# Weights in binary64 decoded with one VectorE pass less: the sign carried through ScalarE's parametric ReLU

## The chip, the cores and the metric

One core of a Trainium2 chip runs the whole program. The metric is device time in microseconds (us) of one execution; the kernel before was timed three times. Its engines are called PE (TensorE, matrix products; PEld are its weight loads), ACT (ScalarE), DVE (VectorE), POOL (GpSimd) and SP (SyncE, which here only issues DMAs).

## The reference

Attention in chunks of 64, then a feed-forward layer with a cosine gate. The weights come in binary64 (64-bit floats), the rest in 32-bit floats.

```python
# q, k, v: (8, 8, 576, 64) float32; chunks of 64 along the sequence
scores = scale * q_c @ k_c.T              # per chunk
scores = scores - max(scores)
attn = exp(scores); attn = attn / (sum(attn) + 1e-09)
out = attn @ v_c
x = out as (4608 tokens, 512)
h = x @ w_in                              # w_in (512, 2048) float64
g = h * cos(h)
return (g @ w_out).astype(float32)        # w_out (2048, 512) float64
```

## The kernel before

The 4608 tokens are nine tiles of 512. A tile's attention gives x, held as two parts (a rounded high part and the rest) so that TensorE's fast 32-bit format keeps the precision; weights and g are split in the same way. The feed-forward layer of one tile is 16 segments, one for each block of 128 of the 2048 hidden columns. A segment has two steps on PE: `hidden` (12 matmuls: 4 blocks of 128 inputs, three products of parts each) gives h, and `project` (12 matmuls) adds g times a block of w_out to four sums. `project` runs three segments (LAG) behind `hidden`.

Between them lies `activated`, six instructions on 128x512 numbers: L492 on ACT (the number of whole turns as an integer), L493 on DVE (h less these turns), L494 on ACT (Sin, which is the cosine by its bias), L495 on DVE (times h; this frees the bank of PSUM, of which there are two, so `hidden` of a segment waits for L495 of two segments earlier), L496 on ACT (high part), L497 on DVE (rest).

The weights, 16 blocks of w_in and 16 of w_out (128x512 each, 512 KB), are read by DMA as raw bits and turned into 32-bit floats on the chip, once, in `split_weight`. For each block: L243 on ACT multiplies the upper words, read as 32-bit floats, by 2 to the power -112, which rebases the exponent; L245 on ACT makes the three bits that come from the lower words (tile `half`); a first L238 pass on DVE shifts the upper word left by three, which pushes the sign out at the top, and joins these bits; a second L238 pass takes the sign from the raw upper word again and joins it; L254 on ACT rounds the high part; L259 on DVE subtracts for the rest. The tile `w` and the tile `half` have two buffers each, so a block's first passes wait for the block two before it.

A tile's attention in the first part (`early`): scores on PE (L177, tiles kt, qt), row maxima L317 and subtraction L321 on DVE, Exp on ACT (L371), sums L381 and reciprocal L385 and L386 on DVE, the product with the reciprocal on POOL or DVE (L391), transposes on PE (L400) with a copy on ACT (L406), the product with v on PE, and its split into x by L455 on ACT and L458 on DVE. Exp and Sin need different tables of ACT; a change of table is an ACT_TABLE_LOAD.

The order of the segments is tile 0's first eight, all of tile 1's, tile 0's last eight, and then tile by tile. For the first 32 segments, with the attention of tiles 0, 1 and 2, all decoding and all early DMA issues, the order is not written by hand: every piece of work is entered by `piece` in a list, with its engine, a length, what it follows, and the time at which its data arrives. `in_order` gives each a due time counted back from the matmul steps and tries 1500 random changes of these times; `placed` runs the list through with one piece at a time for each engine, and the order that ends earliest is issued. The engines then run their queues in that order; the real waits are semaphores. In that list the Sin of every segment follows the eight exponentials of tiles 0 and 1 (`raised`, L844), and the first one has the length 1.83 for its table. Behind the 32 segments the order is fixed by a loop (L855).

Of the kernel before, what the change touches and what calls it, by code (L numbers as in the profile page):

```python
# [11 lines left out]
F32 = mybir.dt.float32  # L12
# [20 lines left out]

EARLY = 2

BY_CHUNK = []

PAIRED = 9


# [4 lines left out]


PE, ACT, DVE, POOL, SP = range(5)

LONG = 2.0

# [6 lines left out]
def placed(work, after_it, rank):  # L57


    n = len(work)  # L60
    left = [len(w[3]) for w in work]
    ready = [w[4] for w in work]
    can = [[] for _ in range(5)]
    for i in range(n):
        if not left[i]:
            can[work[i][0]].append(i)
    free = [0.0] * 5
    starts = [0.0] * n
    slow = 0.0
    for _ in range(n):  # L70
        best = None
        for e, c in enumerate(can):
            if not c:
                continue
            near = 0.2 + min(max(free[e], ready[i]) for i in c)
            first = None
            for i in c:
                at = max(free[e], ready[i])
                if at <= near:

                    mine = (rank[i] if e != PE or work[i][1] > LONG else -1e9, at, i)
                    if first is None or mine < first:
                        first = mine
            if best is None or first[1] < best[0]:
                best = (first[1], first[2], e)
        at, i, e = best
        length = work[i][1]
        if e == PE:

            if at - free[e] > IDLE:  # L90
                slow = at + IDLE
            if length > LONG:
                length += max(0.0, min(length, slow - at))
        starts[i] = at
        free[e] = at + length
        can[e].remove(i)
        for j in after_it[i]:
            left[j] -= 1

            way = 0.0 if e == PE == work[j][0] and length > LONG else work[i][5] - work[i][1]  # L100
            ready[j] = max(ready[j], free[e] + way)
            if not left[j]:
                can[work[j][0]].append(j)
    return starts
# [38 lines left out]
def attention_then_cos_ffn(ctx: ExitStack, tc, qT, kT, v, w_in, w_out, out, wide):  # L143
# [25 lines left out]
    def kept(ins):  # L169
        tc.keep_in_program_order(ins)  # L170
        return ins
# [43 lines left out]
    def split_weight(name, fc, low):  # L215


        raw, n = w_raw.pop((name, fc))
        made = []

        def w():
            if not made:
                made.append(dec.tile([P, n], F32, name="w"))
            return made[0]

        nothing = lambda: None
        if not wide:
            pieces = [lambda: nc.gpsimd.tensor_copy(w(), raw[:, :n])] + [nothing] * 3
        else:

            both = raw.bitcast(U32)[:, : 2 * n].rearrange("p (n k) -> p n k", k=2)
            lower, upper = both[:, :, 0], both[:, :, 1]

            def joined(first, shift, op0, second):
                bits = w().bitcast(U32)
                kept(nc.vector.scalar_tensor_tensor(  # L238
                    bits, first or bits, shift, second or bits, op0=op0, op1=ALU.bitwise_or
                ))  # L240

            pieces = [
                lambda: kept(nc.scalar.activation(  # L243
                    w(), upper.bitcast(F32), AF.Copy, scale=2.0 ** -(MORE // 8))),
                lambda: kept(nc.scalar.activation(low, lower, AF.Copy, scale=LOWEST)),  # L245
                lambda: joined(None, 3, ALU.logical_shift_left, low),
                lambda: joined(upper, 1 << 31, ALU.bitwise_and, None),
            ]

        def high():  # L250
            o = SHIFT if name == "in" else 0
            parts = wts.tile([P, 2 * n + PAD], F32R, name=f"w_{name}{fc}")
            hi, lo = parts[:, o : o + n], parts[:, o + n : o + 2 * n]
            kept(nc.scalar.copy(out=hi, in_=w()))  # L254
            w_parts[name, fc] = (hi, lo)

        def rest():
            hi, lo = w_parts[name, fc]
            kept(nc.vector.tensor_tensor(lo, w(), hi.bitcast(F32), op=ALU.subtract))  # L259

        return pieces + [high, rest]
# [41 lines left out]
    def scores_early(t, hp, s):  # L303

        qt, kt = queries.pop((t, hp))
        for c in range(NCH):
            cs = slice(c * CH, (c + 1) * CH)
            for h in range(2):
                hs = slice(h * CH, (h + 1) * CH)
                matmul(s[hs, cs], qt[hs, cs], kt[hs, cs], start=True, stop=True)  # L310
        sv = s.rearrange("p (c k) -> p c k", k=CH)
        e = weights_of(t, hp // 2)[:, hp % 2]

        m = att.tile([P, NCH], F32, name="m", bufs=4)

        def largest():
            kept(nc.vector.tensor_reduce(out=m, in_=sv, op=ALU.max, axis=AX.X))  # L317

        def below():
            mb = m.unsqueeze(2).broadcast_to([P, NCH, CH])  # L320
            kept(nc.vector.tensor_tensor(e, sv, mb, op=ALU.subtract))  # L321

        def lowered():
            kept(nc.vector.tensor_scalar(m, m, -SCALE, None, op0=ALU.mult))

        def raised_and_summed():
            z = sums_of(t)[:, hp]
            for c in range(NCH):
                kept(nc.scalar.activation(
                    e[:, c], sv[:, c], AF.Exp, bias=m[:, c : c + 1], scale=SCALE,  # L330
                    accum_out=z[:, c : c + 1],
                ))

        return [largest, below, lowered, raised_and_summed]

    def scores(t, g, banks):

# [259 lines left out]

    work = []

    def piece(eng, length, run, *after, at=0.0, lag=0.15):  # L600
        work.append([eng, length, run, [a for a in after if a is not None], at, length + lag])
        return len(work) - 1

    arrival = [3.6]
# [45 lines left out]
    for i, (name, fc) in enumerate(turn_of):  # L650
        key = ("w", name, fc)
        made[key] = split_weight(name, fc, low_bits[i % 2])
        back = turn_of[i - 2] if i > 1 else None
        u = piece(ACT, 0.52, rest_of(key, 0), split.get(back), at=here[name, fc])
        l = piece(ACT, 0.52, rest_of(key, 1), joined.get(back), at=here[name, fc])
        joined[name, fc] = piece(DVE, 0.6, rest_of(key, 2), u, l)
        w = piece(DVE, 0.6, rest_of(key, 3), joined[name, fc])
        h = piece(ACT, 0.52, rest_of(key, 4), w)
        split[name, fc] = piece(DVE, 0.6, rest_of(key, 5), h)


    x_done = {}
    banks_free = {}
    turned_out = {}

    raised = []

    def early(t):
        s, e, z, q, w, p = {}, {}, {}, {}, {}, {}
        for hp in range(HP):  # L670
# [6 lines left out]
            )  # L677
            m = piece(DVE, 0.6, rest_of(key, 0), s[hp])
            room = turned_out.get((t - 1, hp // 2))
            if (t, hp) in BY_CHUNK:  # L680
                m = piece(DVE, 0.2, rest_of(key, 2), m)
                z[hp] = e[hp] = banks_free[which] = piece(ACT, 1.2, rest_of(key, 3), m, room)
            else:
                banks_free[which] = piece(DVE, 0.6, rest_of(key, 1), m, room)
                e[hp] = piece(ACT, 0.6, lambda hp=hp: exponentials(t, hp), banks_free[which])
            raised.append(e[hp])
        for hp in range(HP):
            if hp in z:
                continue
            z[hp] = piece(DVE, 0.6, lambda hp=hp: total(t, hp), e[hp], z.get(hp - 1))  # L690
        for a in (0, 2):
            i = piece(DVE, 0.45, lambda a=a: inverse(t, a, a + 2), z[a], z[a + 1])
            for hp in (a, a + 1):
                if t or hp < 2:
                    q[hp] = piece(POOL, 1.0, lambda hp=hp: quotient(t, hp, nc.gpsimd), i)
                else:
                    q[hp] = piece(DVE, 0.6, lambda hp=hp: quotient(t, hp), i)
        for hp in range(HP):
            key = ("t", t, hp)
            at = banks_free["a", hp % 2] if t else p.get(hp - 2)  # L700
# [36 lines left out]
    def attend_third(begin):  # L737
        t = 2
        below = []
        for g in range(2):  # L740
# [5 lines left out]
            for h in range(2):  # L746
                m = piece(DVE, 0.6, rest_of(key, 2 * h), s)
                below.append(piece(DVE, 0.6, rest_of(key, 2 * h + 1), m))
                banks_free["a", h] = below[-1]
        x = piece(ACT, 4.4, lambda: exponentials(t), *below)  # L750
        z = [None]
        for hp in range(HP):
            z.append(piece(DVE, 0.6, lambda hp=hp: total(t, hp), x, z[-1]))
        z = piece(DVE, 0.5, lambda: inverse(t), z[-1])
        q = [piece(DVE, 0.6, lambda hp=hp: quotient(t, hp), z) for hp in range(HP)]
        w = None
        for g in range(2):
            pts = []
# [40 lines left out]
    for s in range(STAGE):  # L799
# [39 lines left out]
            made[key] = activated(*order[s], made["h", s])  # L839
            made[key][0]()  # L840
        a = piece(ACT, 0.53, begin_g, hid, given.get(s - 2), lag=0.2)
        sine = 0.55 if s else 1.83
        for i, (eng, length) in enumerate(((DVE, 0.6), (ACT, sine), (DVE, 0.6), (ACT, 0.53), (DVE, 0.6)), 1):
            a = piece(eng, length, rest_of(key, i), a, *([projected.get(s - LAG)] if i == 4 else raised if i == 2 else ()))  # L844
            if i == 3:
                held[s] = a
        given[s] = a
# [75 lines left out]
```

## Time and profile before

| | us |
|---|---|
| median of 3 runs | 864.16 (863.83 to 865.03) |
| the profiled execution | 864.98 |
| its span, first to last instruction | 863.2 |
| PE busy (matmuls) | 844.5, 98% of the span |
| DVE busy | 573.9, 66% |
| ACT busy | 390.5, 45% |
| POOL busy | 8.0, 1% |
| granted TensorE clock, mean | 0.996 |
| DMA: packets' share of 16 engines | 18.7%, mean 67 GB/s |

Busy is time in which at least one instruction of the engine ran. A high share over the span tells which engine is the bound on the whole, not where it stands still: for that the span is cut into stretches, and each gap of PE is put beside what ended it. Two instructions of one engine overlap a little at their ends, so the distance between their starts is shorter than the duration of one. A granted clock of 1 is 2.4 GHz, 0.5 would be 1.2 GHz.

### The profile page before, as it was taken

The numbers are of one execution on the slowest core, as the hardware profiler recorded it, in microseconds if no ns is written. First come the engines' busy times: TensorE is split into PE (matmuls) and PEld (weight loads), VectorE is DVE, ScalarE is ACT, GpSimd is POOL, SyncE is SP. The second block draws the span as 40 slices with busy tenths as digits, with TensorE's granted clock in tenths as the row PEclk, the third lists the DMA queues.
The fourth block names the chain that finished last, engine by engine and source line by source line (L and its number), as shares of the span: only waits on it lengthen the run. The fifth ranks groups of instructions, "written<-read, shape, count | busy, mean of one in ns | idle before, by whom it ended". The sixth has DMA issues, their size and how long they took to land.

```text
span 863.2 us, 14114 instructions
## 1 busy us (share of the span) xinstructions
PE 844.5 (98%) x5792; PEld 694.9 (81%) x5792; DVE 573.9 (66%) x974; ACT 390.5 (45%) x632; POOL 8.0 (1%) x12
## 2 busy tenths in 40 slices
PE   5899999999999999999999999999999999999998
PEld 5677888888888888888888888888888888888886
DVE  6999998854696567665776568645865576644332
ACT  4888975343433335333533353334433353333332
POOL 1020000000000000000000000000000000000000
PEclk9999999999999999999999999999999999999999
DMA  9972200330103000300130010301030010001001
GB/s 345 416 314 97 75 1 1 123 123 2 49 1 123 25 20 31 123 25 2 49 113 15 22 49 19 104 25 50 1 122 25 2 50 25 1 1 49 1 1 49
DMA packets 26560, 57.53 MB, mean 67 GB/s; under 512 B 2944, under 2 KB 2944, under 8 KB 26496
## 3 DMA queue, kind: packets, MB, share of 16 engines
q1 hardware_dynamic: 26496, 56.63, 18.2%
q8 instruction: 45, 0.74, 0.4%
q14 instruction: 19, 0.16, 0.1%
HBM read 46.14 MB, written 10.49 MB: 66 GB/s over the span
## 4 chain that ended last, share of the span: by engine, by line
PE 92%; DMA 5%; DVE 2%; SPq 0%; issue 0%
PE acc L177 45%; PE h L177 43%; PE a L177 4%; DMA w_out<-in_w_out_dram 3%; DMA kt<-in_kT_dram 1%; DMA w_in<-in_w_in_dram 1%; DVE w L238 1%; DVE w_in L259 0%; SPq L174 0%; DVE g_lo L497 0%; DVE g L495 0%; DVE z L381 0%; DVE x L458 0%; DVE w_out L259 0%; DVE g L493 0%; PE a L400 0%
## 5 line engine op out<-in xcount | busy, mean ns | idle before, releaser
L177 PE MATMUL h<-x,w_in 128*128 128x512 f32 x1728 | 416.7, 390 | 1.9 <-DVE g L495 1.7
L177 PEld LDWEIGHTS h<-x,w_in 128*128 128x128 f32 x1728 | 324.7, 188 | 70.2 <-DVE g L495 2.1
L177 PE MATMUL acc<-w_out,g_hi 128*128 128x512 f32 x1152 | 358.2, 392 | 0.0
L177 PEld LDWEIGHTS acc<-w_out,g_hi 128*128 128x128 f32 x1152 | 214.0, 188 | 45.3
L177 PE MATMUL acc<-w_out,g_lo 128*128 128x512 f32 x576 | 224.4, 390 | 0.0
L493 DVE SCALAR_TENSOR_TENSOR g<-g,h 128x512 f32<-128x512 int32 x144 | 98.5, 684 | 138.9 <-ACT g L492 138.2
L492 ACT ACTIVATE g<-h 128x512 int32<-128x512 f32 x144 | 85.7, 595 | 194.8 <-PE h L177 194.3
L497 DVE TENSOR_TENSOR g_lo<-g,g_hi 128x512 fp32r<-128x512 f32 x144 | 99.8, 693 | 74.1 <-ACT g_hi L496 71.0
L496 ACT CAST g_hi<-g 128x512 fp32r<-128x512 f32 x144 | 89.4, 621 | 127.6 <-DVE g L495 81.3
L494 ACT ACTIVATE g<-g 128x512 f32<-128x512 f32 x144 | 91.1, 633 | 121.9 <-DVE g L493 121.8
L495 DVE TENSOR_TENSOR g<-h,g 128x512 f32<-128x512 f32 x144 | 99.3, 690 | 53.0 <-ACT g L494 49.8
L177 PEld LDWEIGHTS acc<-w_out,g_lo 128*128 128x128 f32 x576 | 108.1, 188 | 22.7
L417 DVE STREAM_TRANSPOSE pts<-e 32x256 f32<-32x256 f32 x224 | 97.2, 435 | 3.9
L177 PEld LDWEIGHTS a<-kt,qt 64*64 64x64 f32 x1024 | 18.8, 136 | 8.6 <-issue 6.7
L381 DVE TENSOR_REDUCE z<-e 128x8 f32<-128x512 f32 x36 | 23.8, 678 | 0.9 <-ACT e L371 0.9
L177 PE MATMUL a<-kt,qt 64*64 64x64 f32 x1024 | 21.1, 222 | 3.3 <-issue 1.6
L371 ACT ACTIVATE e<-e 128x1024 f32<-128x1024 f32 (+1 forms) x22 | 19.1, 897 | 10.5 <-DVE e L321 10.4
L238 DVE SCALAR_TENSOR_TENSOR w<-w,half 128x512 uint32<-128x512 uint32 x32 | 22.8, 712 | 0.0
L458 DVE TENSOR_TENSOR x<-a,x 128x512 fp32r<-128x512 f32 (+1 forms) x36 | 22.0, 653 | 0.5 <-ACT x L455 0.5
L177 PEld LDWEIGHTS a<-pts,vt 64*64 64x64 f32 x1056 | 17.2, 136 | 5.6 <-issue 4.6
L391 DVE TENSOR_TENSOR e<-e,z 128x512 f32<-128x512 f32 x30 | 20.2, 683 | 0.0
L362 DVE TENSOR_TENSOR e<-a,m 128x512 f32<-128x512 f32 x28 | 19.2, 686 | 0.5
(52 smaller groups left out, 269.5 us busy)
## 6 DMA issues: line engine op xcount, KB each, us to landing
qt<-in_qT_dram SPq DMA_DIRECT2D x36, 256.0 KB, 5.0
kt<-in_kT_dram SPq DMA_DIRECT2D x36, 256.0 KB, 5.3
vt<-in_v_dram SPq DMA_DIRECT2D x34, 256.0 KB, 3.4
w_in<-in_w_in_dram SPq DMA_DIRECT2D x16, 512.0 KB, 9.7
w_out<-in_w_out_dram SPq DMA_DIRECT2D x16, 512.0 KB, 10.0
out_dram<-w SPq DMA_DIRECT2D x16, 256.0 KB, 2.1
out_dram<-half SPq DMA_DIRECT2D x16, 256.0 KB, 2.0
out_dram<-x SPq DMA_DIRECT2D x4, 256.0 KB, 2.0
```

The lines of the kernel that those rows point to most:

```text
L177: kept(nc.tensor.matmul(*args, **kw))
L238: kept(nc.vector.scalar_tensor_tensor(bits, first or bits, shift, second or bits, op0=op0, op1=ALU.bitwise_or))
L381: kept(nc.vector.tensor_reduce(out=sums_of(t)[:, hp], in_=weights_of(t, hp // 2)[:, hp % 2], op=ALU.add, axis=AX.X))
L391: kept(eng.tensor_tensor(e, e, zb, op=ALU.mult))
L417: kept(nc.vector.transpose(out=dst[o : o + BL, :, qb], in_=src[i : i + BL, :, kb]))
L458: kept(nc.vector.tensor_tensor(lo, xq, hi.bitcast(F32), op=ALU.subtract))
L492: lambda: kept(nc.scalar.activation(n, h, AF.Identity, bias=0.25, scale=0.5 / math.pi)),
L493: lambda: kept(nc.vector.scalar_tensor_tensor(g, n, -2.0 * math.pi, h, op0=turns, op1=over)),
L494: lambda: kept(nc.scalar.activation(g, g, AF.Sin, bias=0.5 * math.pi)),
L495: lambda: kept(nc.vector.tensor_tensor(g, h, g, op=ALU.mult)),
L496: lambda: kept(nc.scalar.copy(out=g_hi, in_=g)),
L497: lambda: kept(nc.vector.tensor_tensor(g_lo, g, g_hi.bitcast(F32), op=ALU.subtract)),
```

## The change

The first ACT pass on the upper words becomes a parametric ReLU (Prelu) with the slope minus 2 to the power 32 for negative numbers. A negative weight comes out positive and with 32 added to its exponent, which sets a bit of the exponent that is free here. The shift by three then brings this bit to the place of the sign. So one pass of DVE joins everything, and the second L238 pass goes, for each of the 32 blocks.

The list of pieces changes too. Every entry gets two more fields. `table` names the table (Exp or Sin); `placed` adds 1.28 where a piece needs another than the one held. `port` marks work of POOL and DVE passes with two operands in SBUF; `placed` lets none of one engine start before the last of the other ends. The wait of the Sins on `raised` goes, with the fixed 1.83 and the 4.4 for tile 2's exponentials (now 1.92). An unused branch (`BY_CHUNK` is empty) is taken out.

```diff
 def placed(work, after_it, rank):
+    taken = {DVE: 0.0, POOL: 0.0}
+    table = AF.Exp
+    def soonest(e, i):
+        at = max(free[e], ready[i])
+        if work[i][6]:
+            at = max(at, taken[POOL if e == DVE else DVE])
+        return at
...
-            near = 0.2 + min(max(free[e], ready[i]) for i in c)
+            near = 0.2 + min(soonest(e, i) for i in c)
...
         length = work[i][1]
+        if work[i][7]:
+            length += TABLE * (work[i][7] != table)
+            table = work[i][7]
...
+        if work[i][6]:
+            taken[e] = free[e]
...
-            def joined(first, shift, op0, second):
+            def joined():
                 bits = w().bitcast(U32)
                 kept(nc.vector.scalar_tensor_tensor(
-                    bits, first or bits, shift, second or bits, op0=op0, op1=ALU.bitwise_or
+                    bits, bits, 3, low, op0=ALU.logical_shift_left, op1=ALU.bitwise_or
                 ))
             pieces = [
                 lambda: kept(nc.scalar.activation(
-                    w(), upper.bitcast(F32), AF.Copy, scale=2.0 ** -(MORE // 8))),
+                    w(), upper.bitcast(F32), AF.Prelu, scale=2.0 ** -(MORE // 8), alpha=-(2.0**32))),
                 lambda: kept(nc.scalar.activation(low, lower, AF.Copy, scale=LOWEST)),
-                lambda: joined(None, 3, ALU.logical_shift_left, low),
-                lambda: joined(upper, 1 << 31, ALU.bitwise_and, None),
+                joined,
             ]
...
+    def piece(eng, length, run, *after, at=0.0, lag=0.15, port=False, table=None):
+        port = port or eng == POOL
...
-        joined[name, fc] = piece(DVE, 0.6, rest_of(key, 2), u, l)
-        w = piece(DVE, 0.6, rest_of(key, 3), joined[name, fc])
-        h = piece(ACT, 0.52, rest_of(key, 4), w)
-        split[name, fc] = piece(DVE, 0.6, rest_of(key, 5), h)
+        joined[name, fc] = piece(DVE, 0.6, rest_of(key, 2), u, l, port=True)
+        h = piece(ACT, 0.52, rest_of(key, 3), joined[name, fc])
+        split[name, fc] = piece(DVE, 0.6, rest_of(key, 4), h, port=True)
...
-        sine = 0.55 if s else 1.83
-        for i, (eng, length) in enumerate(((DVE, 0.6), (ACT, sine), (DVE, 0.6), (ACT, 0.53), (DVE, 0.6)), 1):
-            a = piece(eng, length, rest_of(key, i), a, *([projected.get(s - LAG)] if i == 4 else raised if i == 2 else ()))
+        for i, (eng, length) in enumerate(((DVE, 0.6), (ACT, 0.55), (DVE, 0.6), (ACT, 0.53), (DVE, 0.6)), 1):
+            a = piece(eng, length, rest_of(key, i), a, *([projected.get(s - LAG)] if i == 4 else ()), port=i == 5, table=AF.Sin if i == 2 else None)
```

The products L391 on DVE are marked `port=True` as well, and the pieces with Exp (`early`, `attend_third`) get `table=AF.Exp`.

## Rows read from the trace of the kernel before

**Rows 1.** Windows: us, then busy of each engine (instructions), granted clock, DMA.
```profile
20.00:75.00 55.00, 47.70 (x470) 38.80 (x463) 53.30 (x89) 46.80 (x83) 5.22 (x4) 0.97 0.84 336
...
75.00:120.00 45.00, 45.00 (x258) 37.11 (x257) 44.65 (x74) 42.08 (x72) 0.00 (x0) 1.00 0.11 37
...
200.00:840.00 640.00, 640.00 (x4222) 526.43 (x4221) 397.65 (x676) 250.72 (x396) 0.00 (x0) 1.00 0.11 38
```
**Rows 2.** Timeline of PE: start, us, instruction, count; in brackets idle before, releaser.
```profile
28.64 6.85 PE L177 MATMUL h<-x,w_in 128*128 128x512 f32 x24
37.17 5.75 PE L177 MATMUL h<-x,w_in 128*128 128x512 f32 x24 [1.68 <-DVE g L495]
...
66.76 1.06 PE L400 MATMUL a<-ident,e 128*128 128x128 f32 x8 [2.11 <-DVE x L458]
```
**Rows 3.** Chain that ended last: start, us, what.
```profile
74.65 2.72 PE h L177 x12
```
**Rows 4.** Timeline of ACT, 33 to 37 us.
```profile
33.28 0.62 ACT L371 ACTIVATE e<-e 128x512 f32<-128x512 f32 x1
...
34.47 1.28 ACT L494 ACT_TABLE_LOAD   x1
35.77 0.63 ACT L494 ACTIVATE g<-g 128x512 f32<-128x512 f32 x1
```
**Rows 5.** Timeline of DVE, 22 to 37 us.
```profile
22.72 0.69 DVE L259 TENSOR_TENSOR w_in<-w,w_in 128x512 fp32r<-128x512 f32 x1
...
28.25 0.41 DVE L458 TENSOR_TENSOR x<-acc,x 128x256 fp32r<-128x256 f32 x1
...
29.30 1.29 DVE L238 SCALAR_TENSOR_TENSOR w<-w_in,w 128x512 uint32<-128x512 uint32 x2
30.51 0.68 DVE L317 TENSOR_REDUCE m<-a 128x8 f32<-128x512 f32 x1
...
36.43 0.69 DVE L495 TENSOR_TENSOR g<-h,g 128x512 f32<-128x512 f32 x1 [0.40 <-ACT g L494]
```
**Rows 6.** Groups over the span: count | busy us, mean ns | idle before.
```profile
L238 DVE SCALAR_TENSOR_TENSOR w<-w_in,w 128x512 uint32<-128x512 uint32 x16 | 11.5, 722 | 0.1
L238 DVE SCALAR_TENSOR_TENSOR w<-w_out,w 128x512 uint32<-128x512 uint32 x16 | 11.0, 687 | 0.3
```
**Rows 7.** Groups of DVE, 18 to 35 us (one row), 37.2 to 65.3 us (two rows).
```profile
L238 DVE SCALAR_TENSOR_TENSOR w<-w_in,w 128x512 uint32<-128x512 uint32 x4 | 2.7, 686 | 0.0
...
L238 DVE SCALAR_TENSOR_TENSOR w<-w_in,w 128x512 uint32<-128x512 uint32 x4 | 3.3, 827 | 0.0
L238 DVE SCALAR_TENSOR_TENSOR w<-w_out,w 128x512 uint32<-128x512 uint32 x3 | 2.1, 688 | 0.1
```
**Rows 8.** Groups of ACT, 20 to 75 us.
```profile
L243 ACT ACTIVATE w<-w_out 128x512 f32<-128x512 f32 x8 | 5.4, 674 | 0.0
L494 ACT ACTIVATE g<-g 128x512 f32<-128x512 f32 x8 | 5.1, 633 | 0.6 <-DVE g L493 0.6
...
L492 ACT ACTIVATE g<-h 128x512 int32<-128x512 f32 x8 | 4.8, 596 | 1.6 <-PE h L177 1.5
...
L496 ACT CAST g_hi<-g 128x512 fp32r<-128x512 f32 x7 | 4.4, 623 | 1.8 <-DVE g L495 1.8
L243 ACT ACTIVATE w<-w_in 128x512 f32<-128x512 f32 x6 | 4.0, 669 | 0.3 <-DVE w_in L259 0.3
...
L494 ACT ACT_TABLE_LOAD x1 | 1.3, 1283 | 0.0
```
**Rows 9.** Timeline of POOL (first two) and DVE.
```profile
12.78 2.04 POOL L391 TENSOR_TENSOR e<-e,z 128x512 f32<-128x512 f32 x2 [11.48 <-DVE z L386]
...
61.55 2.72 POOL L391 TENSOR_TENSOR e<-e,z 128x512 f32<-128x512 f32 x2 [5.41 <-DVE z L386]
...
63.29 1.53 DVE L259 TENSOR_TENSOR w_in<-w,w_in 128x512 fp32r<-128x512 f32 x1
...
65.34 1.27 DVE L458 TENSOR_TENSOR x<-a,x 128x512 fp32r<-128x512 f32 x2
```

More of the change, by code (lines that the diff above doesn't have):

```diff
@@ L34 @@
 EARLY = 2
-BY_CHUNK = []
 PAIRED = 9
@@ L47 @@
 PE, ACT, DVE, POOL, SP = range(5)
+TABLE = 1.28
 LONG = 2.0
@@ L74, in placed @@
                 continue
-            near = 0.2 + min(max(free[e], ready[i]) for i in c)
+            near = 0.2 + min(soonest(e, i) for i in c)
             first = None
             for i in c:
-                at = max(free[e], ready[i])
+                at = soonest(e, i)
                 if at <= near:
@@ L227, in split_weight @@
         if not wide:
-            pieces = [lambda: nc.gpsimd.tensor_copy(w(), raw[:, :n])] + [nothing] * 3
+            pieces = [lambda: nc.gpsimd.tensor_copy(w(), raw[:, :n])] + [nothing] * 2
         else:
@@ L321, in below @@
             kept(nc.vector.tensor_tensor(e, sv, mb, op=ALU.subtract))
[L323 to L334, printed above, removed]
+        return [largest, below]
     def scores(t, g, banks):
@@ L598, in attention_then_cos_ffn @@
     work = []
-    def piece(eng, length, run, *after, at=0.0, lag=0.15):
-        work.append([eng, length, run, [a for a in after if a is not None], at, length + lag])
+    def piece(eng, length, run, *after, at=0.0, lag=0.15, port=False, table=None):
+        port = port or eng == POOL
+        work.append([eng, length, run, [a for a in after if a is not None], at, length + lag, port, table])
         return len(work) - 1
@@ L664, in attention_then_cos_ffn @@
     turned_out = {}
-    raised = []
     def early(t):
@@ L679, in early @@
             room = turned_out.get((t - 1, hp // 2))
[L680 to L686, printed above, removed]
+            banks_free[which] = piece(DVE, 0.6, rest_of(key, 1), m, room)
+            e[hp] = piece(ACT, 0.6, lambda hp=hp: exponentials(t, hp), banks_free[which], table=AF.Exp)
         for hp in range(HP):
-            if hp in z:
-                continue
             z[hp] = piece(DVE, 0.6, lambda hp=hp: total(t, hp), e[hp], z.get(hp - 1))
@@ L696, in early @@
                 else:
-                    q[hp] = piece(DVE, 0.6, lambda hp=hp: quotient(t, hp), i)
+                    q[hp] = piece(DVE, 0.6, lambda hp=hp: quotient(t, hp), i, port=True)
         for hp in range(HP):
@@ L749, in attend_third @@
                 banks_free["a", h] = below[-1]
-        x = piece(ACT, 4.4, lambda: exponentials(t), *below)
+        x = piece(ACT, 1.92, lambda: exponentials(t), *below, table=AF.Exp)
         z = [None]
@@ L754, in attend_third @@
         z = piece(DVE, 0.5, lambda: inverse(t), z[-1])
-        q = [piece(DVE, 0.6, lambda hp=hp: quotient(t, hp), z) for hp in range(HP)]
+        q = [piece(DVE, 0.6, lambda hp=hp: quotient(t, hp), z, port=True) for hp in range(HP)]
         w = None
```

## The prediction

> **What bounds the kernel now.** I read the windows table first, because a mean over 863 us hides stages [rows 1]. From 200 to 840 us PE is busy 640.00 us of 640 at a granted clock of 1.00 (2.4 GHz): whatever VectorE (398 us) or ScalarE (251 us) does there costs nothing, and the tail behind it decodes no weight. So a gain can only come from the start. From 20 to 75 us PE is busy 47.7 of 55 us while VectorE is busy 53.3 and ScalarE 46.8. From 75 to 120 us VectorE is again full (44.65 of 45), but PE is full too, at full clock: the two engines run ahead there, and their work is not late. The stretch to argue from is 20 to 75 us.
>
> Next the timeline of PE, for its gaps, each with what ended it [rows 2]. h of segments 0 and 1 runs from 28.64 us in 6.85 us (two steps at full clock are 5.44 us, by the 2.72 us step of [rows 3]). PE then stands still for 1.68 us, until VectorE's L495 frees a bank at 37.1 us. The next long gap is 2.11 us, ends at 66.76 us, and is put down to VectorE's L458. From there to the tail the chain is steps of 2.72 us end to end. So what the change moves in time for the step at 74.65 us moves the end by as much, if no new gap opens behind it.
>
> Last, what stands behind the first gap, read backwards. L495 at 36.43 us needs the first Sin at 35.77 us, this needs its table (34.47 us, 1.28 us), and in the list of pieces this first Sin waits for all eight exponentials of tiles 0 and 1; the last of them runs at 33.28 us [rows 4]. That one needs L317 at 30.51 us and the L321 behind it, and ahead of these in VectorE's queue stand two sign passes, 1.29 us at 29.30 us, and the last quarter of tile 0's x at 28.25 us [rows 5]. PE had all of h0's weights at 23.4 us (L259 at 22.72 us), but it began at 28.64 us, as the last x came and tile 1's scores had been put ahead. VectorE's order, not DMA, sets the first 37 us.
>
> **The change, part by part.** *Sign passes.* 32 instructions of L238 go, 16 of 722 ns and 16 of 687 ns, 22.5 us of busy time in all [rows 6]. One pass costs its queue 0.60 us (two of them 1.29 us, less 0.69 us for one of such length [rows 5]), so 19.2 us of queue. Four stand in the queue from 18 to 35 us, 2.4 us; the two of 29.30 us, 1.2 us, are directly on the chain above. Between 37.2 and 65.3 us there are 4 + 3 = 7 more, 4.2 us [rows 7]. All behind 75 us are free of effect, being hidden by PE.
>
> *Prelu in place of Copy.* Same count, operands and scale; 32 instructions of ScalarE change their function. No Prelu is in the trace. The nearest rows: the Copy that it replaces, 669 and 674 ns, and the Sin of 633 ns [rows 8]. I take 0.67 us, the same operands being nearest, so nothing; the ends are 0.63 and, as far above, 0.71 us, and 14 of them in the stretch make 0.6 us either way, beside 8.2 us in which ScalarE is idle there (55 less 46.8). A Prelu needing its own table is a rival below.
>
> *The first Sin no longer waits for the exponentials; the list counts table loads itself.* The planner may now put it sooner, at the price of 2 more loads (2.57 us of ScalarE at 1283 ns [rows 8]), or still behind the exponentials. What h2 gains has two ends. The low end is the 1.2 us of passes on the chain. The high end is h0 at 23.4 us with Sin 0 at once: h0 and h1 take 6.85 us at their clock of today and end at 30.3; g0's chain after h0's 3.4 us (L492 0.60, then 0.69, load 1.28, Sin 0.63, 0.69: 3.9 [rows 8]) ends at 30.7; h2 there instead of at 37.17 is 6.5 us. Below nothing: one alternation on the chain, 2.57 less 1.2, 1.4 us lost. I take 3.0 us: the four sign passes (2.4 us, the chain being VectorE's queue for nearly all of it) plus some 0.6 us, one place in that queue, from L317, L321 and the late x no longer standing behind decoding work.
>
> *VectorE and GpSimd kept apart.* While GpSimd runs its pair of products from 61.55 us, a VectorE subtraction takes 1.53 us in place of 0.69, and the pair itself 2.72 us, not 2.04 as at 12.78 us [rows 9]. The list now starts no two-operand pass of VectorE beside it. Worth at the second gap: from 0.84 us saved ahead of L458 at 65.34 us to the same lost, if nothing else is ready for VectorE meanwhile. I take nothing.
>
> *The second gap.* VectorE reaches L458 4.2 us sooner by its 7 passes, PE needs it 3.0 us sooner by the first term. 1.2 us of difference come off 2.11; I take 1.0, as ScalarE feeds the same x (ends 0 and 2.1). What is late next there is ScalarE: a segment with two new weights costs it nine instructions, some 5.4 us at 0.60, against PE's 5.44.
>
> *The rest* (removed dead branch, lengths in the list for tile 2, number of empty pieces) issues nothing else on a queue, SP's loads included; the order of tile 2's exponentials and the partial sums may move, under a PE that is full from 75 us. Nothing.
>
> Sum: 3.0 + 1.0 = 4.0 us. The profiled execution took 864.98 us (span 863.2 and 1.78 around it), so 861.0; the median of the three runs is 0.82 us lower, 864.16, and the forecast made against it is 860.2 us.
>
> **The rivals.** *Larger* (0.16): h0 at 23.4 us and the whole 6.5 us, the second gap giving little (0.5): 857 us. For it: PE had its weights at 23.4 us, and the granted clock of 0.97 from 20 to 75 us would come back as its early gaps go. Against: ScalarE is 85% busy from 20 to 75 us and would have 8.2 us to spare for being 7 us ahead.
>
> *ScalarE takes over* (0.18): it loses no instruction. If it lets VectorE's time go to waste, only the 1.2 us on the chain stay: 863.0 us, no change. The same comes out of 3.0 + 1.0 with one alternation of tables on the path (2.57 us): 862.7 us. For it: 42.1 of 45 us busy from 75 us on. Against: of its idle 8.2 us, 1.8 end at L495, the largest share [rows 8].
>
> *Table loads, on the slower side* (0.05): from 20 to 75 us there are 14 Copies to be replaced and 8 Sins, and 1 load. If a Prelu is held by neither Exp's nor Sin's table, each Sin is followed by a load for the next Prelu and then one for itself: up to 16 loads, 20.5 us. ScalarE's 8.2 idle us hide six; from the seventh on PE waits; at 16 it is 12.3 us more, 876.5 us. Against: the Copy, casts and Identity run between Sins without a load in the trace, and these loads are only charged in the list for Exp and Sin.
> The Trainium skill, ScalarE: Activation LUTs (Table sets: the hidden batching unit), names relu, copy, identity and abs as in every set, and does not name the parametric one; its section What ACT_TABLE_LOAD costs gives 2.66 us for a switch, drain included. By that price 16 loads would come to 42.6 us and the time to 898.5 us. The trace disagrees on the drain: load at 34.47, Sin at 35.77 us, 1.30 us in all [rows 4].
>
> *The stretched order, slower* (0.07): tile 1's four products on GpSimd bar VectorE's two-operand passes for 4 x 1.02 us in the list; if nothing fills that, the x of tile 1 comes later than PE, now ahead, wants it, and the gap of 2.11 us grows by up to 4.1: less the 2.4 us of passes on the first chain, 865.9 us. It decides once more than 2.4 us of these 4.1 stay empty.
>
> **How the numbers follow.** Forecast 0.54, with its own range 858.4 to 862.3; larger 0.16; ScalarE 0.18; table loads 0.05; order 0.07. What a measurement of this kernel can tell from no change is about 0.2%, 1.7 us: faster is below 862.4, slower above 865.9. Faster 0.54 + 0.16 = 0.70; same 0.18; slower 0.05 + 0.07 = 0.12. The range runs from 856.5 (0.06 of the larger case lies below) to 864.8 (the two slower cases above, 0.12).
>
> **What would show it.** Right: 32 L238-like passes left, 32 Prelus of about 0.67 us, one table load from 20 to 75 us or at most three, h2 at 33 to 35 us, the step that was at 74.65 us starting near 70.6 us, VectorE below 95% from 20 to 75 us. Wrong: h2 at 36 us or later; PE gaps that now end at ScalarE (g_hi, pts, the weights' casts); loads between Sins; a gap of more than 2 us before tile 1's third transpose.

## The result: 0.2% slower, and the profile after

The changed kernel took 867.1 us (median of 20 runs, 865.39 to 868.54) against 865.14 us for before in the same runs: a ratio of 1.0021, 95% interval 1.0014 to 1.0028. The forecast was 860.2 us with a range up to 864.8, and faster. The profiled execution took 865.84 us, span 864.1 us, 0.9 us longer than before's 863.2. It is the third quickest of the 20; the rest of the 1.96 us between the two medians lies in executions that left no trace.

The first 75 us went as forecast, and better. Timeline of PE in the changed kernel (start, us, instruction; L193 is the old L177, L405 the old L400, L463 the old L458, L500 the old L495):

```profile
24.93 3.03 PE L193 MATMUL h<-x,w_in 128*128 128x512 f32 x12
...
28.97 3.02 PE L193 MATMUL h<-x,w_in 128*128 128x512 f32 x12
...
33.00 5.75 PE L193 MATMUL h<-x,w_in 128*128 128x512 f32 x24
...
60.69 1.22 PE L405 MATMUL a<-ident,e 128*128 128x128 f32 x8 [0.66 <-DVE x L463]
```

h of segment 0 begins 3.7 us sooner than in [rows 2], h2 is at 33.00 us, not 37.17, without a gap, and the second gap is 0.66 us, not 2.11. The chain has the step of [rows 3] (`hidden` of segment 8) at 68.69 us, 5.96 us sooner:

```profile
68.69 2.72 PE h L193 x12
```

The windows show where that went (columns as in [rows 1]). VectorE is down from 53.3 to 47.9 us from 20 to 75 us, PE up from 47.7 to 52.5. ScalarE is up from 46.8 to 52.55 us there. But from 120 to 200 us PE stands still for 4.84 us, and the granted clock of the stretch is 0.98; before had 80.00 of 80 us busy there (last row).

```profile
20.00:75.00 55.00, 52.45 (x492) 42.81 (x490) 47.87 (x81) 52.55 (x93) 4.77 (x4) 1.00 0.85 337
75.00:120.00 45.00, 45.00 (x316) 36.73 (x315) 40.06 (x66) 39.54 (x73) 0.00 (x0) 1.00 0.11 36
120.00:200.00 80.00, 75.16 (x442) 61.47 (x441) 49.99 (x90) 31.16 (x49) 0.00 (x0) 0.98 0.20 66
```
```profile
120.00:200.00 80.00, 80.00 (x529) 65.80 (x528) 59.67 (x106) 36.18 (x58) 0.00 (x0) 1.00 0.20 67
```

The gap stands in PE's timeline, with the steps ahead of it. The first row is tile 2's product with v (its first half), the next two are the last two hidden steps of tile 1:

```profile
147.62 1.16 PE L193 MATMUL a<-pts,vt 64*64 64x64 f32 x64
148.71 3.02 PE L193 MATMUL h<-x,w_in 128*128 128x512 f32 x12
...
154.30 2.88 PE L193 MATMUL h<-x,w_in 128*128 128x512 f32 x12
...
164.74 4.44 PE L193 MATMUL h<-x,w_in 128*128 128x512 f32 x12 [4.84 <-DVE g L500]
```

After the gap a step takes 4.44 us, not 2.72, at a granted clock of 0.65 for these microseconds (window, columns as above):

```profile
164.70:169.10 4.40, 4.36 (x12) 3.23 (x12) 3.30 (x6) 1.25 (x3) 0.00 (x0) 0.65 0.00 0
```

That is 1.72 us more. So 4.84 + 1.72 = 6.56 us are given back of 5.96, and some 0.3 us in small places make the 0.9 us of the spans.

What held L500 is read on ScalarE's timeline (L460 is the old L455, L497 to L502 are the old L492 to L497):

```profile
147.86 0.62 ACT L501 CAST g_hi<-g 128x512 fp32r<-128x512 f32 x1 [0.81 <-DVE g L500]
155.63 1.08 ACT L460 CAST x<-a 128x512 fp32r<-128x512 f32 x2 [7.15 <-PE h L193]
156.59 1.23 ACT L497 ACTIVATE g<-h 128x512 int32<-128x512 f32 x2
162.47 0.63 ACT L499 ACTIVATE g<-g 128x512 f32<-128x512 f32 x1 [4.66 <-DVE g L498]
```

The cast of tile 2's x has its input at 148.8 us, when the product ends. It starts at 155.63 us, in the middle of tile 1's last hidden step, and that step is named as what ended 7.15 us of idle time. `x_room` gives tile 2 the buffers named `x1`, where tile 1's x stands: the new x can be written only when the last hidden step of tile 1 has read the old one (the second experiment tests that this is the wait). L497 of segment 22 was ready at 151.7 us and stood behind the cast. VectorE's queue has its counterpart, two L463 and eight transposes, ahead of the L498 that L497 feeds. The chain of waits from there (start, us, what):

```profile
154.46 1.15 PE h L193 x5
...
156.11 0.60 ACT x L460
...
157.89 0.69 DVE x L463
...
161.75 0.69 DVE g L498
...
163.40 0.69 DVE g L498
164.08 0.61 DVE g L500
```

In before these two steps of PE stood the other way round. The last hidden step of tile 1 came first, and the product with v behind it:

```profile
158.72 2.88 PE L177 MATMUL h<-x,w_in 128*128 128x512 f32 x12
161.53 1.16 PE L177 MATMUL a<-pts,vt 64*64 64x64 f32 x64
```

The list of pieces has no edge for this wait. The search moved tile 2's attention 14 us forward (161.53 to 147.62), in front of the step that it has to wait for. With the new list and the old two passes (an experiment below) it did not: there the product stands behind the step, which begins at 157.77 us:

```profile
160.58 1.16 PE L193 MATMUL a<-pts,vt 64*64 64x64 f32 x64
```

### The profile page after: what moved, and what is told of

Read it like the earlier page. It is cut to its first block, busy times and chain, and to the rows that moved or that the text cites. A ratio compares the mean times of both kernels' runs of the same rounds, so it can differ in the third digit from the quotient of the medians.

```text
span 864.1 us, 14053 instructions
## 1 busy us (share of the span) xinstructions
PE 845.4 (98%) x5792; PEld 695.1 (80%) x5792; DVE 555.0 (64%) x942; ACT 389.5 (45%) x636; POOL 7.5 (1%) x12
## 4 chain that ended last, share of the span: by engine, by line
PE 92%; DVE 1%; issue 0%; ACT 0%
PE acc L193 45%; PE h L193 43%; PE a L193 4%; DVE pts L422 1%; DVE x L463 0%; DVE g L498 0%; PE a L405 0%; DVE x L561 0%; ACT x L460 0%; DVE g L500 0%
## 5 line engine op out<-in xcount | busy, mean ns | idle before, releaser
L193 PE MATMUL h<-x,w_in 128*128 128x512 f32 x1728 | 417.2, 390 | 4.8 <-DVE g L500 4.8
L193 PEld LDWEIGHTS h<-x,w_in 128*128 128x128 f32 x1728 | 324.9, 188 | 72.8 <-DVE g L500 5.3
L193 PE MATMUL acc<-w_out,g_hi 128*128 128x512 f32 x1152 | 358.4, 392 | 0.0
L193 PEld LDWEIGHTS acc<-w_out,g_hi 128*128 128x128 f32 x1152 | 214.0, 188 | 45.5 <-ACT pts L559 0.3
L193 PE MATMUL acc<-w_out,g_lo 128*128 128x512 f32 x576 | 224.4, 390 | 0.0
L498 DVE SCALAR_TENSOR_TENSOR g<-g,h 128x512 f32<-128x512 int32 x144 | 98.6, 685 | 143.4 <-ACT g L497 142.5
L497 ACT ACTIVATE g<-h 128x512 int32<-128x512 f32 x144 | 85.8, 596 | 195.2 <-PE h L193 194.8
L502 DVE TENSOR_TENSOR g_lo<-g,g_hi 128x512 fp32r<-128x512 f32 x144 | 99.6, 691 | 75.3 <-ACT g_hi L501 73.1
L500 DVE TENSOR_TENSOR g<-h,g 128x512 f32<-128x512 f32 x144 | 99.5, 691 | 53.7 <-ACT g L499 50.6
L193 PEld LDWEIGHTS acc<-w_out,g_lo 128*128 128x128 f32 x576 | 108.1, 188 | 22.8
L463 DVE TENSOR_TENSOR x<-a,x 128x512 fp32r<-128x512 f32 (+1 forms) x36 | 22.3, 654 | 7.7 <-ACT x L460 7.7
L193 PEld LDWEIGHTS a<-kt,qt 64*64 64x64 f32 x1024 | 18.3, 135 | 7.4 <-issue 5.6
L193 PE MATMUL a<-kt,qt 64*64 64x64 f32 x1024 | 20.6, 221 | 1.6 <-DVE x L463 1.6
L193 PEld LDWEIGHTS a<-pts,vt 64*64 64x64 f32 x1056 | 17.3, 137 | 6.0 <-issue 4.6
L460 ACT CAST x<-a 128x512 fp32r<-128x512 f32 (+1 forms) x36 | 18.5, 565 | 7.7 <-PE h L193 7.2
```

The costliest lines, as they stand in the source:

```text
L193: kept(nc.tensor.matmul(*args, **kw))
L463: kept(nc.vector.tensor_tensor(lo, xq, hi.bitcast(F32), op=ALU.subtract))
L497: lambda: kept(nc.scalar.activation(n, h, AF.Identity, bias=0.25, scale=0.5 / math.pi)),
L498: lambda: kept(nc.vector.scalar_tensor_tensor(g, n, -2.0 * math.pi, h, op0=turns, op1=over)),
L500: lambda: kept(nc.vector.tensor_tensor(g, h, g, op=ALU.mult)),
L502: lambda: kept(nc.vector.tensor_tensor(g_lo, g, g_hi.bitcast(F32), op=ALU.subtract)),
```

## The experiments

Two theories were put against each other. Theory A: the wait on the shared buffer, unknown to the list, is the whole of the late loss. Theory B: the late gap comes from the two engines having been left behind by the reordering, and the buffer is incidental. Ratios are to before in the same runs, with 95% intervals. The runs were made in three sets on three chips, so across sets the ratios are compared, not the times.

**The edge entered in the list.** Tile 2's casts are gathered in `attend_third`; at the last hidden step of tile 1 the edge is entered for each.

```diff
+                into_x.append(hi)
...
+        if s == GROUP + NFC - 1:
+            for i in into_x:
+                work[i][3].append(hid)
```

> The changed kernel, with one more edge in the list of pieces: the casts of tile 2's x follow the last hidden step of tile 1, whose x stands in the same buffers. Theory A (the list does not know this wait; ScalarE's queue stands 7.15 us at the head behind it, and PE loses a gap of 4.84 us and 1.72 us at a lower clock): the casts come behind that step, the gap goes, nothing earlier changes; 867.1 less 6.6 is 860.5 us (859.5 to 862). Theory B (VectorE and ScalarE are simply behind with tile 2's transposes and table loads, the buffer is incidental): a gap of some 4 to 5 us comes back near by, 866 to 868 us.

Measured: 859.5 us, 0.9921 (0.9907 to 0.9934). PE is busy 80.00 of 80 us from 120 to 200 us; the cast comes at 157.84 us, behind the step, with the product with v where it was (147.69 us). That nothing earlier would change was wrong: the edge gave the search another order from the start (h2 at 31.98 us, not 33.00, and a gap of 0.94 us at 53 us). So this run alone doesn't tell the buffer from the order.

```profile
120.00:200.00 80.00, 80.00 (x471) 65.94 (x470) 53.12 (x94) 33.41 (x53) 0.00 (x0) 1.00 0.20 66
```

```profile
157.35 0.60 ACT L497 ACTIVATE g<-h 128x512 int32<-128x512 f32 x1 [1.40 <-PE h L193]
157.84 0.58 ACT L460 CAST x<-a 128x512 fp32r<-128x512 f32 x1
```

**The order kept, the buffer free.** This tells them apart. The last two hidden steps of tile 1 read tile 0's x, so these two segments compute other numbers.

```diff
-            x_hi, x_lo = (x[:, cc % 2] for x in x_parts[t, cc // 2])
+            from_t = 0 if t == 1 and fc >= NFC - 2 else t
+            x_hi, x_lo = (x[:, cc % 2] for x in x_parts[from_t, cc // 2])
```

> The changed kernel in its own order; the last two hidden steps of tile 1 read tile 0's x instead of tile 1's (so these two segments compute other numbers; same instructions, shapes and count). Tile 1's buffers are then free before tile 2's x is written. Theory A: with no instruction moved ScalarE's idle 7.15 us at the cast goes and PE's gap of 4.84 us with it; 860.5 us (859.5 to 862). Theory B: the gap stays within 1 us, 866 to 868 us.

Measured: 860.51 us, 0.9931 (0.9919 to 0.9943). In ScalarE's timeline the same cast starts as soon as its product ends (lines from L480 on are one number higher here):

```profile
147.93 0.62 ACT L502 CAST g_hi<-g 128x512 fp32r<-128x512 f32 x1 [0.81 <-DVE g L501]
148.88 1.07 ACT L460 CAST x<-a 128x512 fp32r<-128x512 f32 x2 [0.33 <-PE a L193]
```

The idle time goes from 7.15 to 0.33 us and PE's late gap is gone, with every instruction in its place:

```profile
120.00:200.00 80.00, 80.00 (x470) 65.97 (x469) 52.68 (x93) 33.35 (x53) 0.00 (x0) 1.00 0.20 66
```

The span is 857.7 us, 6.4 us less than the changed kernel's. Theory A is shown, theory B is out: both kernels end near 860 us.

**The passes alone, in the order of before.** The list is the old one, the second pass an empty piece.

```diff
-                    w(), upper.bitcast(F32), AF.Copy, scale=2.0 ** -(MORE // 8))),
+                    w(), upper.bitcast(F32), AF.Prelu, scale=2.0 ** -(MORE // 8), alpha=-(2.0**32))),
...
-                lambda: joined(upper, 1 << 31, ALU.bitwise_and, None),
+                nothing,
```

> The list of pieces and so every queue's order as before; only the decoding changes on the chip (Prelu, one joining pass; the second pass is an empty piece). Theory A (the passes are worth time from 20 to 75 us even in the old order, and that order has tile 2's x late enough): VectorE's queue is shorter by 4 passes ahead of the first gap and by 7 ahead of the second, 862 us (861 to 863.5) against 865.1 for before, no gap near 160 us. Rival (the early gain comes from the new order alone): 864.5 to 865.5 us.

Measured: 861.71 us, 0.995 (0.9936 to 0.9964), span 858.9. PE's two gaps:

```profile
35.17 5.75 PE L177 MATMUL h<-x,w_in 128*128 128x512 f32 x24 [1.72 <-DVE g L495]
...
62.39 1.06 PE L400 MATMUL a<-ident,e 128*128 128x128 f32 x8 [0.20 <-DVE x L458]
```

h2 comes 2.0 us sooner and the second gap falls from 2.11 to 0.20 us: 3.9 us by the passes alone, about the forecast's whole sum. The span is 4.3 us shorter; the first two hidden steps also take 5.74 us, not 6.85.

**The new list alone, with the old two passes entered in it.**

> The new list (tables, port, no wait of the Sins on the exponentials) with the old decoding in two passes, each entered in the list. Theory A (the first Sin's wait and the passes both hold h2): h2 comes 2 to 3 us sooner than before by the order, but VectorE stays full from 20 to 75 us, 863 us (862 to 865). Rival (the list's freedom alone gives the early gain, the passes none): h2 near 33 us and 859 to 861 us.

Measured: 863.23 us, 0.9962 (0.9949 to 0.9976). The time is as theory A has it, but not by its way: h2 is at 36.53 us, 0.6 us sooner, and the gap at tile 1's third transpose is 1.36 us. `hidden` of segment 0 begins 1.75 us sooner, at 26.89 us, but the first two steps take 7.71 us, not 6.85; the granted clock is 0.94 from 20 to 75 us, in the slowest of the five executions. The new list alone is worth about as much as the passes alone (0.4 and 0.5%), and both together 0.8% once the edge is there.

**The Sins held back again**, with the edge (`raised` of the old list put back).

> The kernel with the edge (859.5 us, 0.992 of before) and every Sin again behind the eight exponentials of tiles 0 and 1, as in the list before. Two table loads at the start of the stretch in place of six. Theory A (the freed Sin gives h2 its early start, worth more than the four loads): h2 comes at 35 us or later, ratio 0.994 to 0.996. Theory C (ScalarE is the bound of the stretch now, 52.5 of 55 us, and the four loads, 5.1 us, are what it pays): h2 a little later but no loads, ratio 0.988 to 0.991.

Measured: 865.27 us, 0.9999 (0.9991 to 1.0008): neither theory. ScalarE has its two table loads and h2 is at 33.86 us, behind a gap of 2.28 us at L500, but PE shows a new wait:

```profile
60.56 1.27 PE L193 MATMUL a<-pts,vt 64*64 64x64 f32 x64 [2.33 <-DMA vt<-in_v_dram]
61.76 4.61 PE L193 MATMUL h<-x,w_in 128*128 128x512 f32 x12
```

The search had put tile 1's attention early, and its last two v, issued behind the stream of weights, landed 9.3 us after their issue. The list has no arrival time for them. This was entered:

```diff
-                at=here["v", 0, hp] if t == 0 else 0.0, lag=0.35,
+                at=here["v", 0, hp] if t == 0 else arrival[0] + 1.3 if hp == 3 else 0.0, lag=0.35,
```

> The kernel with the edge and every Sin behind the eight exponentials (865.3 us, no gain), with the arrival of tile 1's last two v entered in the list. There PE lost 2.33 us to that DMA and 2.28 us to L500 at h2, and hidden steps of 4.6 us beside gaps. Theory D (a wait that the list does not know is again what eats the gain): no gap at a v any more, ratio 0.993 to 0.996. Theory C' (the Sins held back are what costs, the v is incidental): ratio 0.998 to 1.001.

Measured: 862.03 us, 0.9964 (0.995 to 0.9977), the gap at the v gone. So entering a second wait that the list didn't know gave back 0.35%, the way theory D has it and just outside its range; the whole order changed with it, so how much of this is the v alone is not shown. Against the kernel with only the first edge (0.9921) this one is 0.4% behind: h2 stands at 35.69 us, not 31.98, and PE waits 1.47 us for GpSimd's products and 1.71 us for L500. That letting the first Sin go is worth its four extra loads is thus likely; the orders differ in more than the Sins.

**Another draw of the search**, with the edge (seed 2).

> The kernel with the edge, with another seed for the 1500 random trials of the list; the same work. How much of a result is the draw of the search: if the order is settled by its constraints, within 0.002 of the kernel with the edge (ratio 0.990 to 0.994 to before); if the draw decides, more than 0.003 off.

Measured: 860.46 us, 0.9939 (0.9925 to 0.9952): 0.0018 from the kernel with the edge, within 0.002, but only just, and by one other draw. A difference of this size between two orders can be the draw's. Whether another draw without the edge would have missed the late wait by itself was not run.

**Casts of w_out on VectorE**, with the edge.

```diff
-            kept(nc.scalar.copy(out=hi, in_=w()))
+            kept(nc.vector.tensor_copy(hi, w()) if name == "out" else nc.scalar.copy(out=hi, in_=w()))
```

> The kernel with the edge, with the high part of the 16 blocks of w_out cast on VectorE in place of ScalarE (entered so in the list). Theory C (ScalarE is what is late from 20 to 75 us, VectorE has 6.6 us to spare): some 6 casts, 3.6 us, leave ScalarE there; 1 to 2 us faster than with the edge alone, ratio 0.990 or less. Theory A alone (the stretch is bound by the chain through tile 0's x and by PE): no change, 0.992.

Measured: 857.68 us, 0.9908 (0.9895 to 0.9922); the profile's span is 855.7 us against 857.7 with the edge alone. From 20 to 75 us PE is busy 53.35 us. Group of VectorE in that stretch (count | busy us, mean ns):

```profile
L270 DVE CAST w_out<-w 128x512 fp32r<-128x512 f32 x8 | 3.4, 424 | 0.2
```

A cast takes 424 ns there, 631 on ScalarE in the changed kernel. The 0.13% by which this beats the edge alone lies within overlapping intervals and is less than the other draw's 0.18%, so neither theory C nor its rival is shown. It was run once more with the arrival of the v entered as well:

> The kernel with the edge and the w_out casts on VectorE (857.7 us, 0.9908), with a second thing that the list does not know entered too: the last two v of tile 1 can only land behind the stream of weights. PE's order comes out the same, so by every theory within 0.001 of 0.9908; a second measurement of the best version, in other runs.

Measured: 857.76 us, 0.9908 (0.9894 to 0.9921). The two runs agree; this is the lowest ratio measured, and it beats both kernels.

**Two passes in the order made for one.**

> The kernel with the edge, its order kept, but each block decoded by Copy and two joining passes as before, the second directly behind the first (the list is told of one). What the 32 passes are worth where the order doesn't make room for them: theory A: 14 passes up to 75 us at 0.60 us, 8.4 us of VectorE, of which it has 6.6 us idle, so 2 to 6 us slower than with the edge, 862 to 866 us. Rival (with ScalarE as the bound, VectorE's passes are hidden): within 1 us, 859 to 861 us.

Measured: 879.25 us, 1.0152 (1.0137 to 1.0167), some 20 us behind the kernel with the edge where 2 to 6 were expected. ScalarE's casts of the weights now wait for the second pass (groups of ScalarE over the span; L258 is that pass):

```profile
L273 ACT CAST w_in<-w 128x512 fp32r<-128x512 f32 x16 | 9.9, 618 | 7.8 <-DVE w L258 7.8
L273 ACT CAST w_out<-w 128x512 fp32r<-128x512 f32 x16 | 9.9, 616 | 6.5 <-DVE w L258 6.4
```

That is 14.2 us of idle time in the middle of its queue, 3.7 with the edge alone, with Sins and casts of g behind. From 20 to 200 us PE is busy 166.1 us, not 177.2, and the granted clock of the three stretches there is 0.91 to 0.96, not 1.00. That the casts are what PE waits for in the end is argued, not shown. The same passes, known to the list, were 0.9962. So of the 20 us some 16 are the order that doesn't know, with the lower clock behind its gaps, and not the passes.

## Why the prediction was wrong, step by step

- *Sign passes and second gap*: right. The passes alone gave 2.0 us at h2, where 2.4 of the 3.0 stood for them, and 1.9 at the second gap, where 1.0 was taken.
- *Prelu*: right. 32 instructions of 673 ns against 669 and 674 for the Copy [rows 8], and the rival of table loads fell: ScalarE runs from its load at 29.68 us to that at 45.38 us with six Prelus and four Sins and no other load, and five earlier Prelus (10.72 to 26.45 us) stand among the Exps. The Trainium skill, ScalarE: Activation LUTs (Table sets: the hidden batching unit), doesn't name Prelu among what every set holds. Here it ran under either table without a load of its own.
- *The first Sin*: the sign right, the size low: 4.2 us at h2 with the passes, where 3.0 stood. The new order at the start brought this together with the freed Sin; their shares were not measured apart. The price, at most two more loads forecast, was four (six by 75 us, of 1283 ns each), and ScalarE bore it.
- *VectorE and GpSimd kept apart*: nothing, as taken. On the chip they still meet: a VectorE pass of 1.53 us at 57.10 us falls into GpSimd's pair of 2.72 us at 56.81.
- *The rest* is the step that failed: "the order of tile 2's exponentials and the partial sums may move, under a PE that is full from 75 us. Nothing." It was 6.56 us in the profiled execution. The prediction's first part has the condition "if no new gap opens behind it"; the sum put nothing for it. A full PE in the trace of before showed that no wait lay there in that order, not that none could. The forecast gave the search freedom and 19 us of VectorE, and asked what it would do at the start alone. The rival of a stretched order had the right kind (work moved against what PE wants) at the wrong place, with a chance of 0.07. Of the signs that were to show the forecast right, all but the number of loads came true or went further, in a kernel that is slower: none of them looked behind 75 us.
- *The number without the late wait*: 859.5 and 860.5 us stand near the forecast's 860.2 partly by luck. Both were measured beside a before of 866.58 us, so they are 7.1 and 6.1 us below it where 4.0 were forecast, and the early gain in the trace is 5.96 us.

## What to carry to other kernels

When an order comes out of a list with edges, a change that frees an engine moves everything, also where the trace shows no wait: look for the waits that the list doesn't hold (reuse of a buffer, arrival of a late DMA) and ask which of them today's order keeps only because an engine is late. Enter them before timing the change; here the same change is 0.2% slower without the edge and 0.8% faster with it (0.6% by the other draw). In engines that run in order, one waiting cast stops all behind it: the 7.15 us were not ScalarE's work but its queue's head.

## What was not expected of the hardware

- A gap of PE can cost more than its length. After 4.84 us of idle the next hidden step took 4.44 us, not 2.72, at a mean granted clock of 0.65, that is, for much of it at the lower of the two levels (1.2 GHz). Not every gap had this price: after the 1.68 us of [rows 2] two steps took 5.75 us, as at full clock.
- The clock varies from run to run. Over the 20 runs of the changed kernel the mean granted clock lay between 0.990 and 0.996, and the time between 868.5 and 865.4 us, as a rule the longer the lower the clock. Without the gap (four runs of the kernel with the edge) it was 0.996 to 0.998 and the times lay within 0.8 us. That the price of the late gap is what varies is likely; one execution left a trace.
- A table load took 1.28 us and no more, here between a Prelu and an Exp:

```profile
44.71 0.66 ACT L260 ACTIVATE w<-w_out 128x512 f32<-128x512 f32 x1
45.38 1.28 ACT L376 ACT_TABLE_LOAD   x1
46.67 0.63 ACT L376 ACTIVATE e<-e 128x512 f32<-128x512 f32 x1
```

  The Trainium skill, ScalarE: Activation LUTs (What ACT_TABLE_LOAD costs), gives 2.66 us for a switch, with a drain. The drain is not seen here; the measurement decides.
